# Two pairs of heads in each visit to the array in halves, for scores and for values

## The chip, the cores and the metric

The kernel runs on one core of a Trainium2 chip. Its time is the device time of one execution in microseconds (us). The engines of the core work side by side: TensorE (PE in the profile, with its weight loads as PEld), VectorE (DVE), ScalarE (ACT), GpSimd (POOL) and SyncE (SP, whose queue issues all the transfers here).

## The reference

The program is an attention layer whose heads are mixed before and after the softmax ("talking heads"), followed by two layers of a multilayer perceptron. There are 4 batches, 12 heads, 448 positions and 64 numbers per head.

```python
scores = scale * np.matmul(q, k.transpose(0, 1, 3, 2))
scores = np.einsum('bhij,hg->bgij', scores, w_pre)
scores = scores - np.max(scores, axis=-1, keepdims=True)
attn = np.exp(scores)
attn = attn / (np.sum(attn, axis=-1, keepdims=True) + 1e-09)
attn = np.einsum('bhij,hg->bgij', attn, w_post)
x = np.matmul(attn, v)          # then heads side by side: 1792 x 768
h = x @ w_in;  x = (h * np.cos(h)) @ w_out
h = max(x @ w1, x @ w2, x @ w3);  out = h @ w_out2
```

## The kernel before

**Tiles.** Of each batch, the 448 query rows are cut into four parts of 120, 110, 110 and 110 (`SBLK`); the 16 parts of the four batches are numbered `n`. A part is further cut into blocks of 10 query rows (`RI`), 180 in all, numbered `i`. In a block, 10 rows times 12 heads fill 120 partitions, so that one matmul with a 120 x 120 matrix mixes the heads.

**The steps of a part.** `qk(n, hp)` (line 668) computes the scores of two heads, `hp` being the pair. A head has only 64 numbers to contract over, so the two heads of a pair stand in the two row halves of the array, one matmul each (line 675), and each writes a PSUM bank of its own. A float32 matmul appears in the trace as two instructions, so such a visit has 4 records. `evac` copies each bank to a buffer `s` on ScalarE or VectorE, and `send` (line 687) has SyncE move the 12 heads of the part into a tile `t`, in which the heads of a row stand side by side. The scores of part `n` are computed while the blocks of part `n-1` are worked on.

**The steps of a block.** `thigh` and `tlow` cut the float32 scores into two parts `th` and `tl`; the cut's subtraction, `tlow` (line 698), goes to VectorE or to GpSimd. `mix1` is three matmuls (lines 703 to 705), `rowmax`, `soft`, `guard`, `recip` and `wscale` are the softmax, the last writing the scaled mixing matrix `w2s` (line 726). `mix2` is four float32 matmuls, 8 records (line 731), and `keep` copies their result to a tile `a2`.

**The values.** When two parts (a half batch) are done, `av(n, hp)` (line 747) multiplies with V for a pair of heads: four steps over the keys, each with one matmul for either head, the two heads now in the two column halves of the array, both in one PSUM bank. That is 16 records on line 753. `keepx` copies the bank to `xs` in two copies, and `out` sends it to memory.

**PSUM.** Scores and values share a ring of four banks (`ps_s` and `ps_x`, two each), taken in turn by `score_psum` (line 661). `mix1` and `mix2` have two banks each of their own. When the last scores have been sent, `ps_x` is closed and its banks go to the perceptron (`open_early`); from then on only the two banks of `ps_s` are left for values.

**What sets the order.** The attention is ordered by a planner (`Plan`, lines 531 to 594). Each step is added with a rank (a due time, in blocks), the engines that can do it with a cost on each (T, A, V, P, D for TensorE, ScalarE, VectorE, GpSimd and the transfer queue), the steps it comes after, and the rings of buffers it takes and frees. The planner repeatedly picks the step of lowest rank among those that can start next, puts it on the engine that would end it first, and issues it; each engine then executes its instructions in that order. Waits on buffers and data are added to the single instructions. A step that takes from a ring is held until the step that took the place `places` entries ago has been freed:

```python
for ring in takes:
    if len(taken[ring]) >= places[ring]:
        last = self.frees[ring, taken[ring][-places[ring]]]
```

The ranks of the scores are `first[n - 1] + 0.5 + 1.5 * hp`, those of the values `last + 2.5 + 1.5 * hp`, where `first` and `last` are block numbers, `mix1` of block `i` has rank `i` and `mix2` has `i + 1.5`. The perceptron (`Mlps`) follows the attention; its first matmuls and weights are planned into the last part of the attention.

Of the kernel before, what the change touches and what calls it, by code (L numbers as in the profile page):

```python
# [16 lines left out]
B, H, S, D = 4, 12, 448, 64  # L17
# [5 lines left out]
JB, JC = 4, 112  # L23
# [22 lines left out]
@with_exitstack  # L46
def talking_heads_mlps(ctx, tc, q, k, v, w_pre, w_post, same_row, w_in, w_out, w1, w2, w3, w_out2, outT):
    nc = tc.nc
    dram = ctx.enter_context(tc.tile_pool(name="dram", bufs=1, space=bass.MemoryType.DRAM))
    xT = dram.tile([DM, NT], F32, name="xT")  # L50

    tp = ctx.enter_context(tc.tile_pool(name="t", bufs=2, side="right", reuse_waits="tile"))
    mlps = Mlps(ctx, tc, xT, tp, w_in, w_out, (w1, w2, w3), w_out2, outT)
    mlps.kept = {(i, f): dram.tile([128, DM], F32, name=f"w{i}_{f}") for i in range(4) for f in range(KC)}
    with tc.manual_schedule(), ExitStack() as att:
        behind = attention(att, tc, q, k, v, w_pre, w_post, same_row, xT, tp, mlps)
    for ins in behind:
        ctx.enter_context(tc.issue_after(ins))
    mlps.rest()
# [537 lines left out]
def attention(ctx, tc, q, k, v, w_pre, w_post, same_row, xT, tp, mlps):  # L597
    nc = tc.nc
# [12 lines left out]
    q = q.rearrange("(b c g d e i) -> b c g d e i", b=B, c=H // 2, g=2, d=2, e=D)  # L611
# [10 lines left out]
    score = [(b, i0, m, m // RI) for b in range(B) for i0, m in SBLK]  # L622
    blocks = [(n, t) for n, x in enumerate(score) for t in range(x[3])]
    first = [blocks.index((n, 0)) for n in range(len(score))]
    N, NS = len(blocks), len(score)
    plan, live = Plan(), {}
# [31 lines left out]
        nc.sync.dma_start(live["v", b, hp], v[b, hp])  # L658


    def score_psum():

        live["turn"] = live.get("turn", -1) + 1
        if mlps.early or live["turn"] % (BUFS["ps_s"] + BUFS["ps_x"]) < BUFS["ps_s"]:
            return ps_s.tile([128, S], F32, name="ps")
        return ps_x.tile([128, S], F32, name="mps")

    def qk(n, hp, _):
        b, _, m, nt = score[n]
        i0 = score[n][1]  # L670
        both = [score_psum(), score_psum()]
        for g, ps in enumerate(both):
            half = slice(64 * g, 64 * g + 64)
            live["s", n, 2 * hp + g] = ps
            nc.tensor.matmul(ps[:m], live["q", b, hp][half, i0:i0 + m], live["k", b, hp][half], start=True, stop=True)

    def evac(n, h, eng):
        m, ps = score[n][2], live["s", n, h]
# [65 lines left out]
        copy(eng, live["a2", half][:, :, :, o:o + RI], live["a", i][:JC])  # L744


    def av(n, hp, _):
        m, a2 = score[n - 1][2] + score[n][2], live["a2", n // 2]
        vt = live["v", score[n][0], hp]
        ps = live["av", hp] = score_psum()  # L750
        for j in range(JB):
            for g in range(2):
                nc.tensor.matmul(ps[64 * g:64 * g + 64, :m], vt[:, j, g, :], a2[:, j, 2 * hp + g, :m],
                                 start=j == 0, stop=j == JB - 1)

    def keepx(n, hp, eng):

# [14 lines left out]
    def add(f, a, rank, engines, after=(), turn=False, **kw):  # L772

        key = f.__name__, *a
        plan.add(key, rank, partial(f, *a), engines, after, behind=before.get(f, ()) if turn else (), **kw)
        if turn:
            before[f] = [key]

    HP, per = H // 2, len(SBLK)


    rank_qk = {}
    for n in range(NS):
        for hp in range(HP):
            rank_qk[n, hp] = (first[n - 1] + 0.5 + 1.5 * hp) if n else -40.0 + hp
    for x in range(3):
        add(wget, (x,), -50.0, {"D": 0.45})
    add(wmix, (0,), -39.0, {"V": 0.8}, [("wget", 0), ("wget", 2)], takes=["s"], frees=[("s", ("wmix", 0))])
    add(wmix, (1,), -39.0, {"V": 0.2}, [("wget", 1), ("wget", 2)])
    for n in range(NS):  # L790
        b, _, m, nt = score[n]
        for hp in range(HP):
            r = rank_qk[n, hp]
            if n % per == 0:
                early = 8.0 if b else 20.0
                add(qget, (b, hp), r - early, {"D": 0.9}, turn=True, takes=["q"])
                add(kget, (b, hp), r - early, {"D": 0.65}, turn=True, takes=["k"])
            last = [("k", ("kget", b, hp)), ("q", ("qget", b, hp))] if n % per == per - 1 else []
            add(qk, (n, hp), r, {"T": 1.04}, [("qget", b, hp), ("kget", b, hp)], turn=True, takes=["ps", "ps"], frees=last)
            for h in (2 * hp, 2 * hp + 1):  # L800
                add(evac, (n, h), r, {"A": 0.424, "V": 0.535}, [("qk", n, hp)], turn=True, takes=["s"], frees=[("ps", ("qk", n, hp))])
                if h == 0:
                    plan.add(("new_t", n), r, partial(new_t, n), {}, [("evac", n, 0)], takes=["t"])
                add(send, (n, h), r, {"D": 0.65}, [("evac", n, h), ("new_t", n)], turn=True, frees=[("s", ("evac", n, h))])


    for i in range(N):
        n, t = blocks[i]
# [4 lines left out]
            frees=[("th", key("thigh")), ("tl", key("tlow"))])  # L813
# [5 lines left out]
        half = n // 2  # L819
        add(mix2, (i,), i + 1.5, {"T": 0.82}, [key("wscale")], turn=True, takes=["ps_t"], frees=[("e", key("soft")), ("w2s", key("wscale"))])  # L820
        start = n % 2 == 0 and t == 0
# [3 lines left out]
    for n in range(1, NS, 2):  # L825
        b = score[n][0]
        last = first[n] + score[n][3] - 1
        start = ("keep", first[n - 1])
        ends = [("keep", i) for i in range(N) if blocks[i][0] in (n - 1, n)]
        for hp in range(HP):  # L830
            r = last + 2.5 + 1.5 * hp
            if n // 2 % 2 == 0:
                add(vget, (b, hp), r - 10.0, {"D": 0.65}, turn=True, takes=["v"])
            add(av, (n, hp), r, {"T": 1.65}, [("vget", b, hp)] + ends, turn=True, takes=["ps"],
                frees=[("a2", start)] + ([("v", ("vget", b, hp))] if n // 2 % 2 else []))
            add(keepx, (n, hp), r, {"A": 0.45, "V": 0.5}, [("av", n, hp)], turn=True, takes=["xs"], frees=[("ps", ("av", n, hp))])
            add(out, (n, hp), r, {"D": 0.45}, [("keepx", n, hp)], turn=True, frees=[("xs", ("keepx", n, hp))])


    FG = mlps.GROUPS  # L840
# [44 lines left out]
    for x in range(2 * FG + 2):  # L885
        a = divmod(x, 2)
        r = r0 + RANK["fw"] + x * RANK["fwgap"]
# [3 lines left out]
    for n in range(2):  # L891
        r = (r0, N - 1)[n] + RANK[("fx", "x1")[n]]
# [62 lines left out]
```

## Time and profile before

| | |
|---|---|
| three runs | 1331.87 us median (1330.43 to 1333.57) |
| profiled execution | 1330.71 us, span 1329.0 us |
| PE busy | 1273.8 us, 96% of the span |
| PEld busy | 1055.8 us, 79% |
| DVE busy | 1029.5 us, 77% |
| ACT busy | 763.5 us, 57% |
| POOL busy | 289.0 us, 22% |
| mean granted TensorE clock | 0.985 of full speed |

The profile gives one execution. Its busy shares are means over stages: a start of about 38 us, the attention to about 503 us, and the perceptron to the end. Matmuls are pipelined and their ends are modelled, so the time from the start of one group of matmuls to the start of the next says more than their durations.

### The profile page before, as it was taken

How to read it: one execution, taken by the hardware profiler on the slowest of the kernel's cores; microseconds unless marked ns; L12 is line 12 of the kernel's file. 1: busy time of each engine (PE TensorE's matmuls, PEld its weight loads, DVE VectorE, ACT ScalarE, POOL GpSimd, SP SyncE). 2: the span in 40 equal slices, each digit the busy share in tenths (PEclk: the TensorE clock that was granted, in tenths of full speed). 3: DMA queues.
4: the chain of work that ended last, by engine and by line, in shares of the span. 5: the costliest groups of instructions: out<-in, count | busy, mean ns of one | idle time of the engine just before them, and what ended most of it. 6: DMA issues, size and time to landing. Idle time of an engine off the chain costs nothing. (4 is left out here: it accounts for less than half of the span.)

```text
span 1329.0 us, 20579 instructions
## 1 busy us (share of the span) xinstructions
PE 1273.8 (96%) x7002; PEld 1055.8 (79%) x7002; DVE 1029.5 (77%) x2180; ACT 763.5 (57%) x1684; POOL 289.0 (22%) x258
## 2 busy tenths in 40 slices
PE   7999999999999989999999999999989999999998
PEld 2677666776777668888988888889989898989998
DVE  1888797887878797999989998989795645966445
ACT  3877676776777677765545555555553445344430
POOL 0000010000101036121201111111116636256350
PEclk7999999999999999999999999999999999999999
DMA  7652444444343335544343444433102212232112
GB/s 206 195 167 89 125 130 141 124 118 128 110 127 108 123 108 169 141 137 138 101 131 108 119 123 120 131 104 90 54 13 72 72 48 72 79 100 72 48 54 83
DMA packets 84766, 145.44 MB, mean 109 GB/s; under 512 B 9174, under 2 KB 67638, under 8 KB 84662
## 3 DMA queue, kind: packets, MB, share of 16 engines
q1 hardware_dynamic: 84661, 144.14, 36.9%
q8 instruction: 55, 0.90, 0.3%
q14 instruction: 50, 0.40, 0.1%
HBM read 84.95 MB, written 20.45 MB: 79 GB/s over the span
## 5 line engine op out<-in xcount | busy, mean ns | idle before, releaser
L190 PE MATMUL ps<-x,w 128*128 128x448 f32 x708 | 265.3, 375 | 26.0 <-DVE r L229 19.1
L192 PE MATMUL ps<-x,w 128*128 128x448 f32 x708 | 261.6, 370 | 2.4 <-DVE x L358 1.2
L191 PE MATMUL ps<-x,w 128*128 128x448 f32 x708 | 261.7, 370 | 0.0
L731 PEld LDWEIGHTS aps<-w2s,e 120*112 120x112 f32 x1440 | 165.0, 177 | 50.0 <-issue 20.0
L190 PE MATMUL ps<-gh,w 128*128 128x448 f32 x528 | 193.4, 366 | 0.0
L191 PE MATMUL ps<-gh,w 128*128 128x448 f32 x528 | 193.1, 366 | 0.0
L192 PE MATMUL ps<-gl,w 128*128 128x448 f32 x528 | 193.0, 365 | 0.0
L731 PE MATMUL aps<-w2s,e 120*112 120x120 f32 x1440 | 180.2, 271 | 7.8 <-DVE w2s L726 4.9
L337 POOL TENSOR_TENSOR w<-wf,w 128x384 fp32r<-128x384 f32 x126 | 139.8, 1133 | 191.0 <-ACT w L336 131.2
L149 POOL TENSOR_TENSOR w<-wf,w 128x384 fp32r<-128x384 f32 x88 | 99.2, 1138 | 367.5 <-ACT w L146 225.5
L190 PEld LDWEIGHTS ps<-x,w 128*128 128x128 f32 x708 | 134.6, 190 | 48.3 <-DVE r L229 27.0
L192 PEld LDWEIGHTS ps<-x,w 128*128 128x128 f32 x708 | 134.6, 190 | 15.2 <-DVE x L358 1.6
L191 PEld LDWEIGHTS ps<-x,w 128*128 128x128 f32 x708 | 134.7, 190 | 11.1 <-POOL w L149 0.2
L709 DVE TENSOR_REDUCE nm<-mps 120x1 f32<-120x448 f32 x180 | 111.5, 620 | 36.6 <-PE mps L705 33.1
L714 ACT ACTIVATE e<-mps,nm 120x448 f32<-120x448 f32 x180 | 114.8, 638 | 40.0 <-DVE nm L709 31.4
L698 POOL TENSOR_TENSOR tl<-t,th 120x448 fp32r<-120x448 f32 x22 | 26.3, 1196 | 438.2 <-ACT th L613 361.2
L331 DVE TENSOR_TENSOR wf<-wf 128x384 f32<-128x384 f32 x72 | 61.0, 856 | 63.6 <-DMA wf<-w 49.7
L336 ACT CAST w<-wf 128x384 fp32r<-128x384 f32 x126 | 61.2, 515 | 80.7 <-PE ps L192 31.9
L192 PEld LDWEIGHTS ps<-gl,w 128*128 128x128 f32 x528 | 99.1, 188 | 8.6
L190 PEld LDWEIGHTS ps<-gh,w 128*128 128x128 f32 x528 | 99.1, 188 | 8.6 <-issue 0.3
L191 PEld LDWEIGHTS ps<-gh,w 128*128 128x128 f32 x528 | 99.1, 188 | 8.3
L613 ACT CAST th<-t 120x448 fp32r<-120x448 f32 x167 | 94.6, 568 | 19.0 <-DMA t<-s 6.1
(102 smaller groups left out, 2272.3 us busy)
## 6 DMA issues: line engine op xcount, KB each, us to landing
t<-s SPq DMA_DIRECT2D x144, 192.5 KB
wf<-w SPq DMA_DIRECT2D x96, 192.0 KB
wraw<-in_w_out_dram SPq DMA_DIRECT2D x44, 384.0 KB
wraw<-in_w_dram SPq DMA_DIRECT2D x36, 384.0 KB
wraw<-in_w_in_dram SPq DMA_DIRECT2D x32, 384.0 KB
t<-s SPq DMA_DIRECT2D x48, 210.0 KB
w<-wf SPq DMA_DIRECT2D x48, 192.0 KB
q<-in_q_dram SPq DMA_DIRECT2D x48, 112.0 KB
```

Source lines behind the costliest of these rows:

```text
L149: nc.gpsimd.tensor_sub(lo, chunks(o["f"]), f32(hi))
L190: mm(w[0], x[0], start=first, stop=False)
L191: mm(w[1], x[0], start=False, stop=False)
L192: mm(w[0], x[1], start=False, stop=last)
L331: f(raw[x], raw[l], raw[r])
L336: nc.scalar.copy(hi, w)
L337: nc.gpsimd.tensor_sub(lo, w, f32(hi))
L613: copy = lambda eng, *a: nc.scalar.copy(*a) if eng == "A" else any_of[eng].tensor_copy(*a)
L698: any_of[eng].tensor_sub(live["tl", i], live["t", n][:P, t, :], f32(live["th", i]))
L709: nc.vector.tensor_reduce(nm, live["m", i][:P], axis=AX.X, op=ALU.max, negate=True)
L714: nc.scalar.activation(e, live["m", i][:P], AF.Exp, bias=live["nm", i], scale=1.0, accum_out=z)
L731: nc.tensor.matmul(ps[:JC, j], live["e", i][:, j * JC:(j + 1) * JC], live["w2s", i], start=True, stop=True)
```

## The change

`qk` and `av` get a number `x` of two pairs instead of the pair `hp`, and loop over both pairs inside one step. So there are 48 steps of scores instead of 96 and 24 steps of values instead of 48; a step of scores takes four banks, a step of values two. In the planner a step of scores waits for q and k of both pairs and its four `evac` wait for the whole step; the ranks of the steps are 3 blocks apart instead of 1.5. The costs are 1.98 for two pairs of scores (1.04 for one before) and 3.25 for two pairs of values (1.65 for one). The planner's cost of a `send` goes from 0.65 to 0.85. The transfers of q, k and v for two pairs get the same rank.

```diff
+    def pairs(x):
+        return 2 * x, 2 * x + 1
...
-    def qk(n, hp, _):
+    def qk(n, x, _):
...
+        for hp in pairs(x):
+            both = [score_psum(), score_psum()]
+            for g, ps in enumerate(both):
...
-    def av(n, hp, _):
+    def av(n, x, _):
...
+        for hp in pairs(x):
+            vt = live["v", score[n][0], hp]
+            ps = live["av", hp] = score_psum()
...
-            rank_qk[n, hp] = (first[n - 1] + 0.5 + 1.5 * hp) if n else -40.0 + hp
...
+            r = (first[n - 1] + 0.5 + 3.0 * x) if n else -40.0 + 2 * x
+            for hp in pairs(x) if start else ():
                 early = 8.0 if b else 20.0
...
-            add(qk, (n, hp), r, {"T": 1.04}, [("qget", b, hp), ("kget", b, hp)], turn=True, takes=["ps", "ps"], frees=last)
...
+            add(qk, (n, x), r, {"T": 1.98}, [(f, b, hp) for f in ("qget", "kget") for hp in pairs(x)], turn=True, takes=["ps"] * 4,
...
-                add(send, (n, h), r, {"D": 0.65}, [("evac", n, h), ("new_t", n)], turn=True, frees=[("s", ("evac", n, h))])
+                add(send, (n, h), r, {"D": 0.85}, [("evac", n, h), ("new_t", n)], turn=True, frees=[("s", ("evac", n, h))])
...
-            r = last + 2.5 + 1.5 * hp
-            if n // 2 % 2 == 0:
...
-            add(av, (n, hp), r, {"T": 1.65}, [("vget", b, hp)] + ends, turn=True, takes=["ps"],
...
+            r = last + 2.5 + 3.0 * x
+            for hp in pairs(x) if n // 2 % 2 == 0 else ():
...
+            add(av, (n, x), r, {"T": 3.25}, [("vget", b, hp) for hp in pairs(x)] + ends, turn=True, takes=["ps"] * 2,
...
+            for hp in pairs(x):
+                add(keepx, (n, hp), r, {"A": 0.45, "V": 0.5}, [("av", n, x)], turn=True, takes=["xs"], frees=[("ps", ("av", n, x))])
```

## Rows read from the trace of the kernel before

**Rows 1.** Busy time of two stretches: start:end, length, then each engine, clock, transfers.
```profile
75.00:450.00 375.00, 369.55 (x2574) 262.15 (x2573) 304.20 (x860) 270.99 (x677) 19.90 (x17) 1.00 0.41 121
450.00:503.00 53.00, 44.60 (x310) 34.43 (x309) 47.66 (x114) 39.92 (x94) 16.38 (x14) 0.97 0.42 132
```

**Rows 2.** Timeline of PE, no visit between: start, duration, line, count.
```profile
288.81 1.80 PE L731 MATMUL aps<-w2s,e 120*112 120x120 f32 x16
290.38 0.44 PE L703 MATMUL mps<-th,w1h 120*120 120x448 f32 x1
...
291.68 0.98 PE L731 MATMUL aps<-w2s,e 120*112 120x120 f32 x8
```

**Rows 3.** Timeline of PE around one lone pair of scores.
```profile
181.98 0.98 PE L731 MATMUL aps<-w2s,e 120*112 120x120 f32 x8
182.89 1.01 PE L675 MATMUL ps<-k,q 64*110 64x448 f32 x4
...
184.67 0.44 PE L703 MATMUL mps<-th,w1h 120*120 120x448 f32 x1
```

**Rows 4.** Timeline of PE, two pairs of scores in succession.
```profile
364.23 1.01 PE L675 MATMUL mps<-k,q 64*110 64x448 f32 x4
365.08 0.92 PE L675 MATMUL ps<-k,q 64*110 64x448 f32 x4
365.92 0.87 PE L731 MATMUL aps<-w2s,e 120*112 120x120 f32 x6
```

**Rows 5.** Timeline of PE around one lone pair of values.
```profile
162.49 0.44 PE L703 MATMUL mps<-th,w1h 120*120 120x448 f32 x1
...
163.26 1.71 PE L753 MATMUL mps<-a,v 112*64 112x220 f32 x16
164.90 0.46 PE L703 MATMUL mps<-th,w1h 120*120 120x448 f32 x1
...
165.60 0.57 PE L731 MATMUL aps<-w2s,e 120*112 120x120 f32 x4
```

**Rows 6.** Timeline of PE, last values in succession; a window can begin inside a pair.
```profile
497.23 1.84 PE L753 MATMUL ps<-a,v 112*64 112x220 f32 x18
...
498.72 1.84 PE L753 MATMUL ps<-a,v 112*64 112x220 f32 x18
...
501.03 1.71 PE L753 MATMUL ps<-a,v 112*64 112x220 f32 x16 [0.47 <-DVE xs L613]
```

**Rows 7.** Timeline of PE, one pair of values with one of scores behind it.
```profile
204.95 1.80 PE L731 MATMUL aps<-w2s,e 120*112 120x120 f32 x16
206.68 1.77 PE L753 MATMUL ps<-a,v 112*64 112x230 f32 x16
208.39 0.62 PE L675 MATMUL ps<-k,q 64*110 64x448 f32 x1
...
209.33 0.47 PE L703 MATMUL mps<-th,w1h 120*120 120x448 f32 x1
```

**Rows 8.** Timeline of three engines after two pairs of scores, GpSimd subtracting.
```profile
169.20 1.23 DVE L726 TENSOR_SCALAR w2s<-w2t,rz 120x120 f32<-120x120 f32 x1
169.22 1.14 POOL L698 TENSOR_TENSOR tl<-t,th 120x448 fp32r<-120x448 f32 x1 [52.51 <-ACT th L613]
169.51 0.92 PE L675 MATMUL mps<-k,q 64*110 64x448 f32 x4
...
170.58 1.04 PE L731 MATMUL aps<-w2s,e 120*112 120x120 f32 x8
171.38 0.44 PE L703 MATMUL mps<-th,w1h 120*120 120x448 f32 x1
...
172.48 1.76 PE L731 MATMUL aps<-w2s,e 120*112 120x120 f32 x15 [0.25 <-DVE z L718]
```

**Rows 9.** Groups of 75 to 450 us: count, busy, mean ns, idle before.
```profile
L698 POOL TENSOR_TENSOR tl<-t,th 120x448 fp32r<-120x448 f32 x17 | 19.9, 1171 | 350.9 <-ACT th L613 273.9 <-DVE w2s L726 37.6 <-DMA t<-s 35.0
```

**Rows 10.** Timeline of ACT in the start, one copy of scores.
```profile
24.09 0.53 ACT L613 COPY s<-ps 110x448 f32<-110x448 f32 x1 [2.07 <-DMA t<-s]
```

More of the change, by code (lines that the diff above doesn't have):

```diff
@@ L666, in score_psum @@
         return ps_x.tile([128, S], F32, name="mps")
-    def qk(n, hp, _):
[L669 to L675, printed above, removed]
+    def qk(n, x, _):
+        b, i0, m, nt = score[n]
+        for hp in pairs(x):
+            both = [score_psum(), score_psum()]
+            for g, ps in enumerate(both):
+                half = slice(64 * g, 64 * g + 64)
+                live["s", n, 2 * hp + g] = ps
+                nc.tensor.matmul(ps[:m], live["q", b, hp][half, i0:i0 + m], live["k", b, hp][half], start=True, stop=True)
     def evac(n, h, eng):
@@ L744, in keep @@
         copy(eng, live["a2", half][:, :, :, o:o + RI], live["a", i][:JC])
-    def av(n, hp, _):
+    def av(n, x, _):
         m, a2 = score[n - 1][2] + score[n][2], live["a2", n // 2]
[L749 to L754, printed above, removed]
+        for hp in pairs(x):
+            vt = live["v", score[n][0], hp]
+            ps = live["av", hp] = score_psum()
+            for j in range(JB):
+                for g in range(2):
+                    nc.tensor.matmul(ps[64 * g:64 * g + 64, :m], vt[:, j, g, :], a2[:, j, 2 * hp + g, :m],
+                                     start=j == 0, stop=j == JB - 1)
     def keepx(n, hp, eng):
@@ L779, in attention @@
     HP, per = H // 2, len(SBLK)
-    rank_qk = {}
-    for n in range(NS):
-        for hp in range(HP):
-            rank_qk[n, hp] = (first[n - 1] + 0.5 + 1.5 * hp) if n else -40.0 + hp
     for x in range(3):
@@ L791, in attention @@
         b, _, m, nt = score[n]
-        for hp in range(HP):
-            r = rank_qk[n, hp]
-            if n % per == 0:
+        start, end = n % per == 0, n % per == per - 1
+        for x in range(HP // 2):
+            r = (first[n - 1] + 0.5 + 3.0 * x) if n else -40.0 + 2 * x
+            for hp in pairs(x) if start else ():
                 early = 8.0 if b else 20.0
@@ L797, in attention @@
                 add(kget, (b, hp), r - early, {"D": 0.65}, turn=True, takes=["k"])
-            last = [("k", ("kget", b, hp)), ("q", ("qget", b, hp))] if n % per == per - 1 else []
-            add(qk, (n, hp), r, {"T": 1.04}, [("qget", b, hp), ("kget", b, hp)], turn=True, takes=["ps", "ps"], frees=last)
-            for h in (2 * hp, 2 * hp + 1):
-                add(evac, (n, h), r, {"A": 0.424, "V": 0.535}, [("qk", n, hp)], turn=True, takes=["s"], frees=[("ps", ("qk", n, hp))])
+            add(qk, (n, x), r, {"T": 1.98}, [(f, b, hp) for f in ("qget", "kget") for hp in pairs(x)], turn=True, takes=["ps"] * 4,
+                frees=[(f, (f + "get", b, hp)) for f in "kq" for hp in pairs(x)] if end else [])
+            for h in range(4 * x, 4 * x + 4):
+                add(evac, (n, h), r, {"A": 0.424, "V": 0.535}, [("qk", n, x)], turn=True, takes=["s"], frees=[("ps", ("qk", n, x))])
                 if h == 0:
                     plan.add(("new_t", n), r, partial(new_t, n), {}, [("evac", n, 0)], takes=["t"])
-                add(send, (n, h), r, {"D": 0.65}, [("evac", n, h), ("new_t", n)], turn=True, frees=[("s", ("evac", n, h))])
+                add(send, (n, h), r, {"D": 0.85}, [("evac", n, h), ("new_t", n)], turn=True, frees=[("s", ("evac", n, h))])
     for i in range(N):
@@ L829, in attention @@
         ends = [("keep", i) for i in range(N) if blocks[i][0] in (n - 1, n)]
-        for hp in range(HP):
-            r = last + 2.5 + 1.5 * hp
-            if n // 2 % 2 == 0:
+        for x in range(HP // 2):
+            r = last + 2.5 + 3.0 * x
+            for hp in pairs(x) if n // 2 % 2 == 0 else ():
                 add(vget, (b, hp), r - 10.0, {"D": 0.65}, turn=True, takes=["v"])
-            add(av, (n, hp), r, {"T": 1.65}, [("vget", b, hp)] + ends, turn=True, takes=["ps"],
-                frees=[("a2", start)] + ([("v", ("vget", b, hp))] if n // 2 % 2 else []))
-            add(keepx, (n, hp), r, {"A": 0.45, "V": 0.5}, [("av", n, hp)], turn=True, takes=["xs"], frees=[("ps", ("av", n, hp))])
-            add(out, (n, hp), r, {"D": 0.45}, [("keepx", n, hp)], turn=True, frees=[("xs", ("keepx", n, hp))])
+            add(av, (n, x), r, {"T": 3.25}, [("vget", b, hp) for hp in pairs(x)] + ends, turn=True, takes=["ps"] * 2,
+                frees=[("a2", start)] + [("v", ("vget", b, hp)) for hp in pairs(x) if n // 2 % 2])
+            for hp in pairs(x):
+                add(keepx, (n, hp), r, {"A": 0.45, "V": 0.5}, [("av", n, x)], turn=True, takes=["xs"], frees=[("ps", ("av", n, x))])
+                add(out, (n, hp), r, {"D": 0.45}, [("keepx", n, hp)], turn=True, frees=[("xs", ("keepx", n, hp))])
     FG = mlps.GROUPS
```

## The prediction

> **What bounds the kernel now.** I read the busy time by stage first, then the timeline of PE in the attention, start to start, then the groups and the waits. In the steady attention (75 to 450 us) PE is busy for 369.55 of 375 us at full clock, DVE for 304.20 (81%), ACT for 270.99 (72%) [rows 1]. Since the ends of matmuls are modelled, the reader should take the starts: two `mix2` and then a `mix1` start 290.38 - 288.81 = 1.57 us apart [rows 2], and these figures repeat over the whole stage to 0.01 us, except at some 20 places. PE streams, and its order of work sets the time. From 450 to 503 us PE is busy for 44.60 of 53 and DVE for 47.66 (90%) [rows 1]: no scores are left to fill PE, and the blocks wait for VectorE. The perceptron behind it has the same instructions after the change, so I let it move as a whole with the attention's end.
>
> The Trainium skill (Perfetto Trace Analysis, Identifying the Most-Contended Engine) calls matmul busy time a bad measure for the room left on TensorE and would take the weight loads' share instead; that is 262.15 of 375 us, 70% [rows 1]. By that rule PE has room, and less work on it buys nothing: the time would stay at 1331.9 us. The starts at equal distance speak against it here.
>
> **What a visit costs, and what the second pair in it costs.** A lone pair of scores: `mix2`, scores, `mix2`, `mix1` take 184.67 - 181.98 = 2.69 us [rows 3], the same without the scores 1.57 [rows 2], so a lone visit costs 1.12 us. Two pairs in succession do occur already: first to second 365.08 - 364.23 = 0.85, second to the next `mix2` 365.92 - 365.08 = 0.84 [rows 4]. One lone pair occupies 0.94 of its 1.12 us between its own first start and the next instruction's (there is one such row behind values: 209.33 - 208.39 = 0.94 [rows 7]), so the second pair adds 0.85 + 0.84 - 0.94 = 0.75. Two pairs in one visit save 1.12 - 0.75 = 0.37 us: the change between full array and halves, in and out, is paid once.
>
> A lone pair of values: `mix1`, values, `mix1`, `mix2` take 165.60 - 162.49 = 3.11 us [rows 5], without values `mix1`, `mix1`, `mix2` take 291.68 - 290.38 = 1.30 [rows 2], so 1.81 us. In succession one pair takes 498.72 - 497.23 = 1.49 [rows 6]. Two pairs in one visit save 0.32 us.
>
> **How many.** Followed along the timeline from 38 to 503 us there are 83 visits for scores (the other 13 of the 96 lie in the start, where PE waits anyway): 48 alone, 12 in six pairs as in rows 4, and 23 beside a visit for values (18 behind one as in rows 7, 5 ahead of one). Of the 48 visits for values 21 are alone, 23 beside scores, and the last four follow one another, of which rows 6 shows three. After the change there are 42 double visits for scores behind the start; six unions exist, so 36 x 0.37 = 13.3 us. For values 24 unions less the 3 that exist, 21 x 0.32 = 6.7 us. Together 20.0 us.
>
> Against it stand the 23 neighbours. Two `mix2`, values, scores and the next `mix1` take 209.33 - 204.95 = 4.38 us [rows 7], less the 1.57 of rows 2 is 2.81. Apart they would cost 1.12 + 1.81, and 0.07 more as these values have 230 columns (208.39 - 206.68 = 1.71, against 164.90 - 163.26 = 1.64 [rows 5]): 3.00. So a neighbour saves 0.19 us already. If all of them go, 23 x 0.19 = 4.4 us are lost; if as many per visit stay, 12 go and 2.3 are lost. The ranks speak for few: scores at 0.5, 3.5 and 6.5 of a part and values at 1.5, 4.5 and 7.5 have a block's `mix1` and `mix2` between them. I take 3.0 lost, and PE saves 17.0 us (15.6 to 17.7).
>
> **What it adds.**
> - The start. The last scores of the first part come with four copies to do in place of two, and the copies of that time wait for buffers that SyncE still has to send (one copy 0.53, the wait ahead of it 2.07 [rows 10]). One more copy on each engine, then one more wait for a buffer at half of that row: 0 to 2.6, I take 1.2 us. The transfers of q and k are the same in number and order of pairs; nothing of them moves past another queue's work.
> - The end of the attention. With two banks left, a double visit fills both, and the next one waits for the copies of the first. The row of today's wait is 0.47 us [rows 6], for one bank. Two boundaries between three visits: 0 to 2 x 0.47, I take 0.9.
> - Banks in the steady stage. A step of scores needs all four banks. The planner's test looks at the holder four places back, four times at the same one; with values between two visits of scores it doesn't see that values still hold two banks, and the matmuls of the second pair would then wait on PE, with every `mix1` and `mix2` queued behind them. The price is again 0.47 to 0, for at most 24 visits of values: 0 to 11.3 us. Ranks put two blocks, some 5 us, between a visit for values and the next for scores, so I take 1.2.
> - Coarser bursts. While PE is in a double visit for values (about 1.64 + 1.49 = 3.1 us) no `mix1` reaches VectorE; the two banks of `mix1` and two sets of `th` and `tl` cover that as long as they are full. On the other side the last scores of a part have rank 6.5 instead of 8 and are sent earlier. PE's idle time of 375 - 369.55 = 5.45 us in the stage [rows 1] is all that can be regained. From -5.45 to +9.5 (the 0.45 of the second wait in rows 8, 1.10 - 0.65, behind half of the 42 visits), I take 1.0 lost.
>
> Sum against the profiled execution: 1330.71 - 17.0 + 1.2 + 0.9 + 1.2 + 1.0 = 1318.0 us. The median of the runs shown is 1331.87, 1.16 above that execution, so I forecast **1319.2 us**.
>
> VectorE is next. Over 375 us it would be busy for the same 304.20 in some 361 us, 84%, still below PE. The Trainium skill (TensorEngine Tiling, PSUM Bottleneck) warns that packing the array speeds up TensorE and not the copies out of PSUM, which may then bound. By that rule the gain would stop where VectorE is full; at 84% it isn't, but the rule is the ground of the second rival below.
>
> **The rivals.**
> - More: nothing is lost and the 5.45 us of waits go with the earlier sends. 1331.9 - 17.0 - 5.45 + 1.2 = 1310.6 us. For it: the planner's costs for the double visits (1.98, 3.25) are near what the rows give (1.12 + 0.75 = 1.87; 1.81 + 1.49 = 3.30), while today's 1.65 for values is 0.16 short, so its order fits PE better. Against it: start and end can only lose.
> - No change: PE's gain is waited away because VectorE and ScalarE get four copies at once. Each of the 66 double visits would have to cost 17.0 / 66 = 0.26 us. Time about 1331. For it: DVE at 81%, 90% in the last stretch [rows 1]. Against it: copies are there in the same number, and two banks stand on either side of `mix1` and `mix2`.
> - Slower: the subtractions move to GpSimd. The planner gives `tlow` to GpSimd when VectorE is booked some 0.7 us ahead (its costs are 1.25 and 0.535), and four copies together book it further than two. While GpSimd subtracts, VectorE's `w2s` takes 1.23 us, and its `mix2` starts late: 170.58 - 169.51 = 1.07 in place of 0.84, and then 172.48 - 171.38 = 1.10 in place of 0.65 (half of the 1.30 above): 0.68 us of PE [rows 8]. There are 17 such subtractions now in the steady stage [rows 9]. It decides from 17.0 / 0.68 = 25 more. One for every second double visit, 33 x 0.68 = 22.4 us, and with the 3.3 us of start, end and banks 1331.9 - 17.0 + 22.4 + 3.3 = 1341 us; one for each, 1363. Against it: not every one of the 17 stops PE, and more time between `mix1` and `mix2` in a double visit hides some.
>
> **How the numbers follow.** Forecast 0.50, with a range of its own from 1313 to 1326; more 0.17; no change 0.16; slower 0.17. The range for 8 in 10 takes in the forecast, nearly all of the first rival, the second, and of the third the cases with a few more subtractions than decide it: 1309 to 1335. A change of 0.2%, 2.7 us, is about what a measurement here can tell from none. Faster: 0.50 + 0.17 and 0.05 of the no-change case, 0.72. Within: 0.08. Slower: 0.17 and 0.03 of the same case, 0.20.
>
> **What would show it.** In the changed trace line 675's successor should have 8 records per visit for scores in about 1.69 us from first start to the next instruction, and the values 32 in about 3.1 us; `mix2` to `mix2` with a visit between should show 0.91 + 1.69. The perceptron should start at about 490 instead of 503 us and last as long as before. The forecast falls if PE's starts show gaps behind the double visits of over 0.26 us on the mean, if GpSimd's count on line 698 is above 40, or if PE is seen waiting for copies of values in the middle of a visit for scores.

## The result, and the profile after

The changed kernel takes 1318.81 us (median, 1317.30 to 1319.01), the kernel before 1331.15 in the same comparison: the ratio is 0.9904 (95% interval 0.9885 to 0.9923). The forecast was 1319.2. Repeated later, the ratio was 0.9908 (0.9891 to 0.9925). The profiled execution took 1319.01 us with a span of 1317.2.

The busy time by stage of the changed kernel, with the columns of [rows 1] (start:end, length, PE, PEld, DVE, ACT, POOL, clock, transfers); the second stretch ends, as in [rows 1], with the attention:

```profile
75.00:435.00 360.00, 352.95 (x2555) 264.46 (x2552) 296.34 (x885) 265.45 (x659) 10.74 (x9) 1.00 0.41 127
435.00:488.40 53.40, 46.80 (x338) 37.71 (x337) 46.97 (x118) 38.46 (x94) 16.43 (x14) 0.97 0.43 133
```

PE is still the engine that is nearly always busy in the steady stage, 98.0% against 98.5% in [rows 1]. The stage does the same work faster: in 360 us PE executes 2555 instructions, where the kernel before needs 375 for 2574. The attention ends at 488.2 us instead of 502.7.

The timeline of PE (start, duration, line, count): one double visit for scores, and the `mix2` behind it.

```profile
74.65 1.01 PE L679 MATMUL ps<-k,q 64*110 64x448 f32 x4
75.49 0.92 PE L679 MATMUL mps<-k,q 64*110 64x448 f32 x4
76.34 1.08 PE L735 MATMUL aps<-w2s,e 120*112 120x120 f32 x8
```

And one for values:

```profile
198.70 3.33 PE L758 MATMUL ps<-a,v 112*64 112x230 f32 x32
201.96 1.89 PE L735 MATMUL aps<-w2s,e 120*112 120x120 f32 x16
```

Two pairs of scores take 76.34 - 74.65 = 1.69 us as in [rows 4], two pairs of values 3.26 with 230 columns. Along the timeline behind the start there are 42 visits of the first kind and 24 of the second; each stands alone between `mix1` and `mix2` (the last three of values between matmuls of the perceptron), and none of the 23 neighbours of before is left.

**Where the 11.8 us of span went.** I took each start-to-start distance on PE apart into the least distance that this kind of instruction has between such neighbours in either trace, and the rest, which I call a wait (what a lower clock costs counts as one too). From the first `mix1` to the last visit for values the least distances add to 439.1 us before and 422.3 after: 16.8 us less to stream. The first `mix1` starts at the same time. The waits are 2.6 us longer (30.0 and 32.6): 2.7 more in the 30 us behind the start, 1.2 more from 75 to 433 us, 1.2 less from there on. That leaves 14.3 us at the end of the attention. The perceptron then takes 2.5 to 2.7 us longer and gives these back: 16.8 - 2.6 - 2.5 = 11.7. The terms of one or two us are rough: telling the neighbours apart more or less finely gives 15 to 18 us for the stream, and each trace is one execution (in the trace of the repeat, run 10, the attention ends at 486.4 us).

The first `mix1`, before and after:

```profile
31.86 0.73 PE L703 MATMUL mps<-th,w1h 120*120 120x448 f32 x1
```
```profile
31.72 0.73 PE L707 MATMUL mps<-th,w1h 120*120 120x448 f32 x1 [0.52 <-DVE th L613]
```

Most of the 2.7 us behind the start comes from one place, here in the timeline of DVE, POOL and PE after:

```profile
50.59 1.22 DVE L730 TENSOR_SCALAR w2s<-w2t,rz 120x120 f32<-120x120 f32 x1
50.60 1.13 POOL L702 TENSOR_TENSOR tl<-t,th 120x448 fp32r<-120x448 f32 x1 [10.72 <-ACT th L613]
...
51.95 1.05 PE L735 MATMUL aps<-w2s,e 120*112 120x120 f32 x8 [1.82 <-DVE w2s L730]
...
52.63 0.28 DVE L730 TENSOR_SCALAR w2s<-w2t,rz 120x120 f32<-120x120 f32 x1
```

PE waits 1.82 us for a `w2s` that takes 1.22 us beside a subtraction on GpSimd. After this wait the granted clock of TensorE falls to the lower of its two levels for a while (1.2 in place of 2.4 GHz): its mean from 38 to 75 us is 0.95 of full speed, against 1.00 before. In the trace of run 10 the same wait is there (1.83 us), and the clock stays at 1.00.

**What waits in place of what.** Waits in the steady stage (75 to 435 us), engine and line, whom it waited for, us in total, times, longest. Before:

```profile
PE mps L703 <- ACT e L714: 1.0, 2, 0.8
...
ACT s L613 <- DMA t<-s: 0.6, 1, 0.6
```

After:

```profile
PE mps L707 <- ACT e L718: 5.1, 10, 1.9
...
ACT s L613 <- DMA t<-s: 4.4, 5, 1.7
...
DVE s L613 <- DMA t<-s: 2.2, 4, 0.7
```

The copies of scores now wait for a buffer `s` that is still being sent. The longest case, timeline of all engines:

```profile
170.94 0.98 PE L735 MATMUL aps<-w2s,e 120*112 120x120 f32 x8
171.69 0.53 ACT L613 COPY s<-mps 110x448 f32<-110x448 f32 x1 [1.70 <-DMA t<-s]
172.12 0.57 ACT L613 CAST th<-t 120x448 fp32r<-120x448 f32 x1
172.59 0.57 ACT L613 COPY a<-aps 112x480 f32<-112x480 f32 x1
172.72 0.62 DVE L702 TENSOR_TENSOR tl<-t,th 120x448 fp32r<-120x448 f32 x1 [2.19 <-ACT th L613]
173.04 0.65 ACT L718 ACTIVATE e<-mps,nm 120x448 f32<-120x448 f32 x1
...
173.83 0.47 PE L707 MATMUL mps<-th,w1h 120*120 120x448 f32 x1 [1.90 <-ACT e L718]
```

Read it from below: PE waits 1.90 us for ScalarE's exponential, which stands behind a copy of `mix2`'s result and a cast, which stand behind a copy of scores that waited 1.70 us for the send of an earlier one. A double visit brings four copies at once, and there are six buffers.

**GpSimd.** Its subtractions in the same stage, to be held against [rows 9]:

```profile
L702 POOL TENSOR_TENSOR tl<-t,th 120x448 fp32r<-120x448 f32 x9 | 10.7, 1194 | 351.4 <-DMA t<-s 267.5 <-ACT th L613 83.9
```

17 became 9 (over the whole kernel 22 became 15).

### The profile page after: what moved, and what is told of

Same layout as the page of the kernel before. It is cut to its first block, busy times and chain, and to the rows that moved or that the text cites. A ratio compares the mean times of both kernels' runs of the same rounds, so it can differ in the third digit from the quotient of the medians.

```text
span 1317.2 us, 20573 instructions
## 1 busy us (share of the span) xinstructions
PE 1257.6 (95%) x7002; PEld 1064.6 (81%) x7002; DVE 1023.6 (78%) x2213; ACT 754.5 (57%) x1659; POOL 279.9 (21%) x250
## 5 line engine op out<-in xcount | busy, mean ns | idle before, releaser
L702 POOL TENSOR_TENSOR tl<-t,th 120x448 fp32r<-120x448 f32 x15 | 18.2, 1210 | 437.6 <-DMA t<-s 305.8
```

What stands on the lines that cost most here:

```text
L702: any_of[eng].tensor_sub(live["tl", i], live["t", n][:P, t, :], f32(live["th", i]))
```

## The experiments

Twelve runs in three groups; the runs of a group shared one chip and the runs of the kernel before. All ratios are to the kernel before, with their 95% interval. Two readings were to be told apart: that PE's way into and out of the halves is what is saved, or that the planner's new costs and due times do it.

**1. Scores alone, 2. values alone.** One of the two steps keeps its loop over single pairs.

```diff
 # scores_only: changed kernel, but
-    def av(n, x, _):
+    def av(n, hp, _):          # with its planning, as in the kernel before
 # values_only: kernel before, but
-    def av(n, hp, _):
+    def av(n, x, _):           # with its planning, as in the changed kernel
```

> Double visits for scores alone; values stay in 48 single visits as in the kernel before. Theory (what is saved is the way into and out of the halves, paid once per visit): 36 new unions x 0.37 = 13.3 us off, less 2 to 4 us for values that no longer stand beside scores, so 1320 to 1324 us, and line 679 shows 42 double visits of 1.69 us behind the start. Rival (the gain comes from values as much as from scores, by bank turns): half of 12.3, about 1325. Rival (planner's costs and due times of the scores do it): all of 12.3, about 1319, with gaps on PE gone and the visits no cheaper.

> Double visits for values alone; scores and the cost of a send stay as before. Theory: 21 unions x 0.32 = 6.7 us off, less up to 23 x 0.19 = 4.4 us of neighbours lost, so 1325 to 1330 us; together with the run of scores alone more than the whole, as each of the two still meets the other's single visits. Rival (values in two banks hold up the next scores): no gain or 1 to 3 us slower, 1331 to 1335.

Scores alone: 1317.11 us, ratio 0.9893 (0.9873 to 0.9912). Values alone: 1326.62 us, 0.9967 (0.9954 to 0.9979). Values came out inside the theory's range; scores gained more than theory allowed, and are level with the whole change. The time is the one that the rival of costs and due times gave, but not under its condition: the trace shows 42 double visits, 38 of them of 1.69 or 1.70 us, so the visits did get cheaper. Values in pairs do shorten the stream (429.5 us of least distances with scores alone, 422.3 with both), and the attention ends 4.6 us earlier with both; but from the start of the last pair of values to the start of the last matmul of the kernel it is 822.2 us with scores alone and 826.7 with both. So the gains of the two halves, 13.9 and 4.4 us, don't add to the 12.3 of the whole. In the attention of the traces they do (scores alone end it 9.9 us earlier than before, values alone 2.2, both 14.5), and with both the perceptron gives some back. This is not all of the 6 us that are missing: the profiled executions were the slowest of either run (1319.05 and 1330.16 us), and the rest stays open.

**3. Costs alone.** The kernel before, planned with costs that fit the rows.

```diff
-            add(qk, (n, hp), r, {"T": 1.04}, ...
+            add(qk, (n, hp), r, {"T": 1.12}, ...
-                add(send, (n, h), r, {"D": 0.65}, ...
+                add(send, (n, h), r, {"D": 0.85}, ...
-            add(av, (n, hp), r, {"T": 1.65}, ...
+            add(av, (n, hp), r, {"T": 1.81}, ...
```

> The kernel before, its single visits kept, with planner costs near what the rows give: a send 0.85, a pair of scores 1.12, of values 1.81. Theory: the time stays within 3 us of before, 1328 to 1334, as the number of visits is the same. Rival (a planner that fits the chip better is where the gain comes from): 1319 to 1325.

1330.36 us, ratio 0.9992 (0.9979 to 1.0004). The rival of better costs falls.

**4. Due times alone.** Each pair stays a step of its own, but two share a rank (and a `send` has the cost 0.85, as in run 3).

```diff
-            rank_qk[n, hp] = (first[n - 1] + 0.5 + 1.5 * hp) if n else -40.0 + hp
+            rank_qk[n, hp] = (first[n - 1] + 0.5 + 3.0 * (hp // 2)) if n else -40.0 + hp // 2 * 2
...
-            r = last + 2.5 + 1.5 * hp
+            r = last + 2.5 + 3.0 * (hp // 2)
```

> The kernel before with the due times of the changed one (two pairs share a rank, 3 blocks apart) and a send at 0.85, but each pair still a step of its own that takes two banks (values one). Theory: the time follows the number of unions that come about by themselves, 0.37 each for scores and 0.32 for values; with two banks free the second pair can follow at once, so I expect about half of them, 1323 to 1328 us. Rival (only one step in the planner keeps pairs together): no unions, 1331. Rival (due times do it all): 1319.

1321.46 us, ratio 0.9937 (0.9918 to 0.9957): somewhat less than the 1323 to 1328 us that I expected, and not for my reason. Only 9 unions of scores and 16 of values came about, all neighbours of values and scores were lost, and the stream is as long as before (437.0 us of least distances against 436.2, the least ones taken over the traces of this and the next groups too). What went are waits: from 75 to 433 us PE waits 6 us instead of 13. Busy time by stage and the subtractions of GpSimd in it:

```profile
75.00:435.00 360.00, 358.77 (x2521) 255.84 (x2520) 278.65 (x828) 273.85 (x695) 3.44 (x3) 1.00 0.42 125
```
```profile
L698 POOL TENSOR_TENSOR tl<-t,th 120x448 fp32r<-120x448 f32 x3 | 3.4, 1147 | 290.4 <-DVE rz L722 290.4
```

GpSimd does 3 subtractions in place of 17 [rows 9], and PE is busy for 99.7% of the stage. So the due times can win some 8 us by themselves, by another mechanism than the change. In the changed kernel itself they win nothing of the kind: its waits are no shorter than before (30.0 and 32.6 us above), and its stream is. Whether the fewer subtractions on GpSimd are that mechanism is looked at in runs 7 and 9.

**5. and 6. The way into and out of the halves, by itself.** One small matmul over the whole array per double visit, between its pairs or ahead of them.

```diff
                 live["s", n, 2 * hp + g] = ps
+                if n > 1 and g == 0 and hp % 2 == 1:   # full_ahead: == 0; the same for values
+                    nc.tensor.matmul(ps[:P, :P], w1l, w1h, start=True, stop=True)
```

> The changed kernel with one more small matmul over the whole array (120 x 120 weights, 120 columns) between the two pairs of each double visit, written to a bank that the second pair then overwrites: 66 of them behind the start. Compared with the same matmul ahead of the visit (next run). Theory: it forces the way out of and into the halves once more, so this run is slower than the next by 42 x 0.37 + 24 x 0.32 = 23 us: about 1345 to 1355 with the matmuls' own 0.05 to 0.2 us each. Rival (order and due times make the gain): the two runs agree within 3 us.

> The changed kernel with the same small matmul ahead of the first pair of each double visit, where PE is on the whole array anyway. Theory: 66 x 0.05 to 0.2 us, so 3 to 13 us over the changed kernel, 1322 to 1332. Rival: as the run with it between the pairs.

Between: 1342.35 us, ratio 1.0063 (1.0039 to 1.0088). Ahead: 1322.97 us, 0.9941 (0.9917 to 0.9964). The same matmul costs 4 us over the changed kernel where PE is on the whole array anyway, and 19.4 us more in the middle of the visits. Timeline of PE for one visit, between:

```profile
76.31 0.37 PE L711 MATMUL mps<-tl,w1h 120*120 120x448 f32 x1
76.60 1.01 PE L681 MATMUL ps<-k,q 64*110 64x448 f32 x4
77.54 0.32 PE L680 MATMUL mps<-w1h,w1l 120*120 120x120 f32 x1
77.79 1.01 PE L681 MATMUL mps<-k,q 64*110 64x448 f32 x4
78.72 1.07 PE L737 MATMUL aps<-w2s,e 120*112 120x120 f32 x8
```

and ahead:

```profile
74.81 0.37 PE L711 MATMUL mps<-tl,w1h 120*120 120x448 f32 x1
75.01 0.22 PE L680 MATMUL ps<-w1h,w1l 120*120 120x120 f32 x1
75.16 1.01 PE L681 MATMUL ps<-k,q 64*110 64x448 f32 x4
76.00 0.92 PE L681 MATMUL mps<-k,q 64*110 64x448 f32 x4
76.85 1.07 PE L737 MATMUL aps<-w2s,e 120*112 120x120 f32 x8
```

From the last `mix1` matmul to the `mix2`: 78.72 - 76.31 = 2.41 us and 76.85 - 74.81 = 2.04. The 0.37 us of the prediction is there once more, and in the other double visits for scores too (0.37 to 0.39). A visit for values with 220 columns takes 3.81 and 3.47 us, 0.34 more. Over the attention the least distances differ by 23.0 us (448.5 and 425.5), near 42 x 0.37 + 24 x 0.32 = 23.2. The medians differ by less, 19.4, and run 5 came out below the 1345 to 1355 us that I expected. Why is open: the profiled execution of run 6 took 1332.03 us, 9 us over the median of its run, so its waits (some 10 us more in the attention than in run 5) don't speak for the others. The same matmul in the same order of work, at two places, costs different time: this shows the mechanism, a break of the run in halves that has to be paid. Whether a matmul of another kind that keeps to the halves would break it too was not run.

**7. No subtraction on GpSimd, in the changed kernel; 9. in the kernel before.**

```diff
-        add(tlow, (i,), i - 1.5, {"V": 0.535, "P": 1.25}, ...
+        add(tlow, (i,), i - 1.5, {"V": 0.535}, ...
```

> The changed kernel with all subtractions of tlow on VectorE, none on GpSimd (15 now). Theory: they are few and mostly hidden now, within 2 us of 1318.8. Rival (while GpSimd subtracts, w2s takes 1.2 us instead of 0.28 and PE waits 0.68 each time): 15 x 0.68 = 10 us faster, 1309. Rival (VectorE is near its limit): 2 to 4 us slower.

> The kernel before with all subtractions of tlow on VectorE (22 on GpSimd before). Theory (each subtraction on GpSimd holds up w2s and through it PE, 0.3 to 0.4 us on the mean, as taking 15 away from the changed kernel gave some 5 us): 7 to 9 us under before, about 1323. Rival (the 5 us came with another order in the changed kernel alone): within 3 us of before, 1331. Rival (the full 0.68 each): 15 us under, 1316.

Changed kernel: 1314.33 us, ratio 0.9856 (0.9830 to 0.9882), against 0.9904 and 0.9908 with GpSimd. Kernel before: 1324.21 us, 0.9943 (0.9927 to 0.9959). The first theory, that the 15 left are hidden, falls, and the full price of 0.68 us each as well: on the mean 0.3 to 0.5 us a subtraction in both kernels ((1332.13 - 1324.21) / 22 = 0.36). The mean of all the `w2s` (columns: count, busy us, mean ns, idle before), before and without GpSimd:

```profile
L726 DVE TENSOR_SCALAR w2s<-w2t,rz 120x120 f32<-120x120 f32 x180 | 57.7, 320 | 3.7
```
```profile
L726 DVE TENSOR_SCALAR w2s<-w2t,rz 120x120 f32<-120x120 f32 x180 | 52.7, 293 | 4.6
```

The 7.9 us that this gives the kernel before are near what the due times gave it in run 4 with 11 subtractions instead of 22; but the count doesn't explain run 4. Run 3 has 11 subtractions on GpSimd too (5 of them from 75 to 435 us) and gained nothing:

```profile
L698 POOL TENSOR_TENSOR tl<-t,th 120x448 fp32r<-120x448 f32 x11 | 13.4, 1218 | 449.2 <-ACT th L613 193.2 <-DMA x<-xT 117.4 <-DMA xT<-xs 106.5
```

So 0.36 us is a mean over all of them, with the new order that the planner makes without GpSimd, and no fixed price; what the due times of run 4 win stays open.

**8. More buffers for the copies.**

```diff
-BUFS = {"k": 10, "q": 9, "s": 6, ...
+BUFS = {"k": 9, "q": 8, "s": 8, ...
```

> The changed kernel with 8 buffers for scores on their way out (s) in place of 6, paid with one buffer of k and one of q. Theory of what is still lost: the third and fourth copy of a double visit wait for a buffer whose send hasn't landed, and with them the steps behind on the same engine; some 5 such waits in the steady stage cost PE 4 to 6 us, so 1313 to 1316. Rival (those waits are hidden, or the lost buffers of k and q cost as much): within 2 us of 1318.8.

1317.29 us, ratio 0.9888 (0.9861 to 0.9914): not told apart from the changed kernel (0.9904, 0.9908). The theory falls for the steady stage. The copies wait less (2.3 us on ScalarE instead of 4.4), yet PE waits as long (14 us), now with 13 subtractions on GpSimd in place of 9. What did move is the start: the first `mix1` stands at 27.90 us instead of 31.72.

**10. The changed kernel again, 11. both edits on it, 12. scores alone without GpSimd.**

```diff
 # no_pool_s8: changed kernel, but
-BUFS = {"k": 10, "q": 9, "s": 6, ...
+BUFS = {"k": 9, "q": 8, "s": 8, ...
-        add(tlow, (i,), i - 1.5, {"V": 0.535, "P": 1.25}, ...
+        add(tlow, (i,), i - 1.5, {"V": 0.535}, ...
```

> The changed kernel once more, on the same chip as the three below. Theory: 12 us under before, 0.990 of it.

> The changed kernel with both: no subtraction on GpSimd and 8 buffers s (9 for k, 8 for q). Theory (two separate waits, VectorE's w2s and the buffers of the copies): the gains add, 5 and 1 to 4 us, so 0.982 to 0.986 of before, 1308 to 1313. Rival (both fill the same gaps of PE): as without the buffers, 0.9856.

> Double visits for scores alone and no subtraction on GpSimd. Theory (the double visits for values save 6.7 us of PE's time less the 3 of lost neighbours, but the run of scores alone was as fast as the whole, so what they save is waited away elsewhere): level with the changed kernel without GpSimd, 1311 to 1316. Rival (values in pairs cost nothing and save their 4 us): 4 us slower than that, 1317 to 1319.

Again: 1318.55 us, 0.9908 (0.9891 to 0.9925). Both edits: **1306.80 us, ratio 0.9827 (0.9806 to 0.9849)**, inside the ratios of the theory and the fastest version, 12 us under the changed kernel. That the two further buffers are worth something without GpSimd's subtractions is likely, not shown: 0.9827 and 0.9856 come from two groups, and their intervals overlap. Its first `mix1` and its two stretches of the attention:

```profile
28.11 0.73 PE L707 MATMUL mps<-th,w1h 120*120 120x448 f32 x1 [1.84 <-DVE th L613]
```
```profile
75.00:427.00 352.00, 345.54 (x2503) 258.94 (x2504) 294.75 (x878) 260.64 (x648) 0.00 (x0) 1.00 0.41 130
427.00:480.40 53.40, 47.91 (x358) 38.68 (x357) 48.71 (x128) 42.95 (x104) 16.33 (x14) 1.00 0.37 112
```

It starts the blocks 3.6 us earlier than the changed kernel and ends the attention at 480.1 us instead of 488.2. Scores alone without GpSimd: 1310.44 us, 0.9846 (0.9827 to 0.9865), level with the whole change without GpSimd (0.9856), as the theory had it. In that pair PE waits 21 us instead of 30 in the attention and streams 7 us longer.

## Why the prediction was right, point by point

- **PE sets the attention's time.** Right. Taking 16.8 us out of PE's stream ended the attention 14.3 us earlier, and putting a way in and out back (runs 5, 6) cost 19.4. The distances repeat less exactly than I wrote: of some 400 from 75 to 450 us, 20 are over their least by more than 0.1 us, but some 90 by more than 0.01.
- **The prices, 0.37 and 0.32 us.** Right; in run 5 against run 6 they were measured by themselves, 0.37 and 0.34.
- **The counts.** 42 and 24 double visits are as forecast. All neighbours went, where I had kept some: the low end, 20.0 - 4.4 = 15.6, was due, I took 17.0. The trace has 16.8, which can't be told from either (15 to 18 us by the reckoning above).
- **The start, 1.2 us.** Mis-sized: 0 up to the first `mix1`. In the next 30 us 2.7 us follow that I hadn't named here: most of it is the price of the slower rival, once (1.82 us for a `w2s` beside GpSimd), and a stretch at 1.2 GHz that the repeat doesn't have.
- **The end of the attention, 0.9 us lost.** Wrong in sign: 1.2 us of waits less there. PE is busy for 46.80 of 53.4 us, against 44.60 of 53 [rows 1]. The wait that I had named stands at one boundary, as long as before (0.45 us, and 0.47 in [rows 6]):

```profile
481.06 3.19 PE L758 MATMUL ps<-a,v 112*64 112x220 f32 x32 [0.45 <-ACT xs L613]
```

- **The banks, 1.2 us.** No wait of PE for copies of values shows in the steady stage: 0.
- **Bursts, 1.0 us.** The size holds (1.2), the place doesn't: I looked at `mix1`'s banks, and what waits are the copies, for buffers of `s`. That these cost PE the 1.2 us is not shown: with half of them gone (run 8) PE waits as long.
- **VectorE.** Forecast 84%, measured 296.34 of 360, 82%: not the bound. The second rival needed 0.26 us a double visit; the waits grew by 2.6 / 66 = 0.04. What the Trainium skill warns of (TensorEngine Tiling (Array Packing), PSUM Bottleneck) did not show here: no engine is full, and the copies' new wait is for buffers still being sent. The rule of the Trainium skill on the room left on TensorE (Perfetto Trace Analysis, Identifying the Most-Contended Engine), as I read it, would have given no change with the weight loads at 70%; the measurement is against this reading. The Trainium skill names a second measure there beside the weight loads' share (MFU, the share of the peak arithmetic), which I left out.
- **The first rival, more.** PE's idle time did not go: it is 360 - 352.95 = 7.05 us from 75 to 435 us, after 5.45 before [rows 1].
- **The slower rival.** Its mechanism is real (runs 7 and 9), its direction was wrong: GpSimd got fewer subtractions, 9 instead of 17, and the price of one is 0.36 us rather than 0.68. Less of it gave the changed kernel a gain that I hadn't forecast; by that price 8 fewer would be 3 us, which is about what the new waits for `s` took. That these two cancel is worked out, not shown, and run 3 speaks against a price by the count.
- **The perceptron moves as a whole.** Wrong by 2.5 to 2.7 us, and in the repeat by 4.2. Part of it stands in one place, where the granted clock is lower (before, then after, then the repeat; the same 70 us of work seen from the attention's end):

```profile
940.00:1010.00 70.00, 66.29 (x319) 60.72 (x318) 56.32 (x98) 36.51 (x70) 13.83 (x13) 0.98 0.15 43
```
```profile
925.73:995.73 70.00, 65.13 (x310) 59.71 (x310) 55.00 (x97) 35.92 (x70) 11.77 (x11) 0.95 0.15 43
```
```profile
923.75:993.75 70.00, 65.12 (x312) 59.64 (x311) 55.45 (x98) 36.05 (x70) 12.11 (x11) 0.95 0.15 43
```

The column ahead of the last two is the clock: 0.95 against 0.98, so more of the stretch lies at 1.2 GHz. In it PE waits for VectorE ahead of one matmul, and the clock falls during that wait or just behind it. Before, then after:

```profile
989.24 0.47 PE L190 MATMUL ps<-x,w 128*128 128x448 f32 x1 [3.71 <-DVE acc L279]
```
```profile
976.94 0.74 PE L190 MATMUL ps<-x,w 128*128 128x448 f32 x1 [4.87 <-DVE acc L279]
```

PE falls 1.7 us further behind there: 4.87 - 3.71 = 1.16 us are a longer wait (4.88 us in the repeat), and the rest is what the clock adds. The other 1.0 us has built up by then and doesn't lie in one place: PE is 1.4 us behind after the first 20 us, where the order of the first matmuls differs, level again some 50 us behind the attention, and 1.0 us behind from 400 us on. Why VectorE is later there stays open; with scores alone the perceptron isn't longer (822.2 us, as above), and no run was made for it.

So the sum came out within 0.4 us of the median because the perceptron's 2.5 us stand about where I had put losses for start, end and banks that didn't come. The mechanism and its size are shown; the closeness of the total is partly chance.

## What to carry to other kernels

When an engine streams, price a reordering from start-to-start distances between the same neighbours, with and without the thing, and look for places where the new order already occurs: two rows gave 0.37 us, and an isolated test gave the same. Count what the present order shares that the new one will not (here the neighbours). And after such a change look at every ring that now gets its work in bursts: the buffers and the engine that the planner picks when another is booked were together worth as much (12 us) as the change itself.

## What the runs showed of the hardware

A matmul of 120 columns over the whole array, put between two pairs of scores in halves, costs 0.37 us more than the same matmul ahead of them (2.41 and 2.04 us). While GpSimd subtracts, VectorE's `w2s` takes 1.22 us in place of 0.28 (as at 50.59 and 52.63 us above). Taking all 22 subtractions off GpSimd made the kernel before 7.9 us faster, 0.36 us each on the mean, though GpSimd itself is nearly idle in the steady stage and VectorE then does the 0.62 us of work that one takes there (as at 172.72 above). It is no fixed price: 11 fewer in run 3 brought nothing.
